# Batch 1 in aligned key sets, one-operation activation for batch 0, global values copied on chip

## The chip, the cores and the metric

One of the eight cores of a Trainium2 chip. The metric is the device time of one execution in microseconds. An execution is timed without the profiler several times; one more is taken with it, and all lines of views come from that one.

## The reference

Eight batches of attention with eight heads of width 64: 512 local tokens see the keys within 32 positions and all 32 global keys; 32 global tokens see everything. The joined result goes through a hidden layer of 2,048 with a sigmoid gate.

```python
k_all = np.concatenate([k_g, k_l], axis=2)
v_all = np.concatenate([v_g, v_l], axis=2)
out_g = np.matmul(sm(scale * np.matmul(q_g, k_all.transpose(0, 1, 3, 2))), v_all)
s_ll = np.where(np.abs(pos[:, None] - pos[None, :]) <= 32, scale * (q_l @ k_l^T), -1e9)
a_l = sm(np.concatenate([scale * (q_l @ k_g^T), s_ll], axis=-1))
out_l = np.matmul(a_l, np.concatenate([v_g, v_l], axis=2))
x = np.concatenate([out_g, out_l], axis=2)      # to tokens x 512
h = x @ w_in                                    # 4352 x 2048
out = (h * (1.0 / (1.0 + np.exp(-1.702 * h)))) @ w_out
```

Inputs and output are float32; the matmuls run on bf16 operands.

## The kernel before

**Units.** A batch is done as two quads of four heads (`a` and `c`). In a quad the four heads lie on the four groups of 32 partitions, so that four score matmuls with 32 rows of contraction stand in the array together, one for each head. Scores go to two pairs of PSUM banks (`psS`), everything else to four banks that go round (`psP`): hidden layer `hp`, output `op`, values `ov`.

**Two forms of attention.** `Quad` (batches 0 and 1) has keys as rows and takes its local scores in four blocks of 128 keys with windows of queries (`WIN`). `S` makes scores, `X` exponentials, `M` multiplies by the near mask (batch 1 only; batch 0 adds a bias in PSUM instead, `B`). The global keys go apart: `K` makes their scores, `XK` the exponentials `ek`, `ekU` their part of the sum. In batch 1's first quad `XK` also makes `ek2`, `ek` with its partition groups turned by one, with two SyncE DMAs (`load_turned`); `rvt` is the global values turned in the same way. Values are the weights of the matmuls in `U`, exponentials the moving side, so the sums come out transposed; `R` turns the row of sums, inverts it and turns it back, `XL` multiplies. `Gm` and `G` do the global tokens.

`Wide` (batches 2 to 7) uses key sets of 128 rows: 96 local keys and the 32 global keys beside them (`spread` copies keys into that layout, on ScalarE; `ext` puts the global ones in). Here the exponentials are the weights and the values move, 66 columns wide with a column of ones (`UG`); `RXG` normalises on VectorE and transposes. Local keys start at three offsets, so the values are needed at three alignments: `vt` as loaded, and two turned copies `vturn`, made by `turn_v` with four SyncE DMAs. `load_v` loads five blocks of 96 local values, each followed by a DMA of the same global values beside it, and a last block of 32.

**Activation.** gelu-like gate as h * (1 + tanh(0.851 h)) / 2: tanh on ScalarE (`th`), then a VectorE operation (th + 1) * hp to `gT`; the factor 0.5 is in the copy of the output (`o_out`). `act4` does the same for 4 steps of batch 0 that wait in the `psS` banks.

**Order.** Written out by hand; every engine runs its instructions in program order. Batch 0's attention; its hidden layer (16 steps `fc` of 4 matmuls); then batch 0's output projection (`osteps`, 16 groups of 4 matmuls) with batch 1's attention between; batch 1's hidden layer with the start of batch 2's attention; then `phase_o(i)` and `phase_h(i)` alternate: output of batch i with attention of batch i+1, hidden layer of batch i+1. Global tokens of all batches come last.

**Loads.** The loads from DRAM that cast to bf16 are issued by GpSimd (POOL) in one queue, in the order of `load_rest`, then `load_v(2)`, then `loads(i)` in hidden layer i. Output copies and turned values are issued by SyncE (SP). `keep` is 28 matmuls on zeros at the start, before there is data.

Of the kernel before, what the change touches and what calls it, by code (L numbers as in the profile page):

```python
# [20 lines left out]
def kernel(  # L21
# [67 lines left out]
    def load_v(b):  # L89
        vt = v_rows(b)  # L90
        if b < 4:
            nc.gpsimd.memset(vt[:, :, :, D:], 1.0)
        vs, vg = (x[b].rearrange("h s d -> s h d") for x in (v_l, v_g))
        for c in range(5):
            nc.gpsimd.dma_start(out=vt[0:96, c, :, :D], in_=vs[96 * c : 96 * c + 96])  # L95
            nc.gpsimd.dma_start(out=vt[96:128, c, :, :D], in_=vg)  # L96
        nc.gpsimd.dma_start(out=vt[0:32, 5, :, :D], in_=vs[480:512])

# [11 lines left out]
    rvg = consts.tile([128, 4, D + 2], BF16)  # L110


    rvt = consts.tile([128, 4, D + 2], BF16)
# [5 lines left out]
    def load_g(lo, hi, names="kqv"):  # L119
        for name, dst, src in (("k", rkg, kgf), ("q", rqg, qgf)):  # L120
            if name in names:
                nc.gpsimd.dma_start(out=dst[:, lo:hi, :], in_=src[:, lo:hi, :])
        if "v" in names:
            load_turned(nc.gpsimd, rvg[:, lo:hi, :D], vgf[:, lo:hi, :])
# [33 lines left out]
    for i in range(2):  # L158
        vtiles.append(consts.tile([128, 8 * 6 * (D + 2)], BF16, name="v%d" % i))
        nc.gpsimd.memset(v_view(i, 4)[:, :, :, :, D:], 1.0)  # L160
# [25 lines left out]
    keep(28, psP.tile([128, 512], F32, name="w", tag="p"), 128)  # L186

    qtiles = []
    for i in range(4):
        qt = consts.tile([128, 24, 32], F32, name="q%d" % i)  # L190
        nc.vector.memset(qt[:, 0:4, :], 0.0)
        nc.vector.memset(qt[:, 20:24, :], 0.0)
        qtiles.append(qt)

    WIN = ((0, 10), (6, 12), (14, 12), (22, 10))
    near_mask = consts.tile([128, 2, LW], BF16)
# [15 lines left out]
    def make_near(c):  # L212
        nr = WIN[c][1]
        at = (0, 160, 0, 192)[c]
        nc.scalar.activation(near_mask[:, c // 2, at : at + 16 * nr].rearrange("p (t r) -> p t r", t=16),
                             near(bandt, c), AF.Copy)

# [5 lines left out]
    def mask_put(g, first, last, by, late):  # L223
# [22 lines left out]
    qgT = consts.tile([128, 4, 40], F32)  # L246
    nc.vector.memset(qgT[:, :, 32:], 0.0)
    kgT = consts.tile([128, 4, 32], F32)
# [12 lines left out]
    def load_rest():  # L261
        load_v2(0)
# [5 lines left out]
        for g4 in (1, 0, 2, 3):  # L268
            nc.gpsimd.dma_start(
                out=w_out_sb[:, 4 * g4 : 4 * g4 + 4, :].rearrange("p (g e) m -> p g (e m)", e=2),  # L270
                in_=w_out_r[:, 2 * g4 : 2 * g4 + 2, :])
            if g4 == 0:
                load(1, (0,))
                load_g(2, 4)
        load(1, (1,))
        load(2, kq=False)
        nc.gpsimd.dma_start(out=loaded[2][1][:, 0], in_=qf[2][:, 0])
        load_g(4, 8, "k")
        load_v2(1)
        load_g(4, 8, "q")  # L280
        nc.gpsimd.dma_start(out=loaded[2][0], in_=kf[2])
        nc.gpsimd.dma_start(out=loaded[2][1][:, 1], in_=qf[2][:, 1])
# [14 lines left out]
    class Quad:  # L297
        def __init__(self, Q):
# [5 lines left out]
            self.v = v_view(self.b, 4 if self.b < 2 else 5)[:, self.u]  # L304
            if self.b < 2:
# [43 lines left out]
        def S(self, rnd, split=False, added=False, part=None):  # L349
# [19 lines left out]
            if not part:  # L369
                self.E[rnd] = att.tile([128, 4, RW + 32], BF16, name="e%d" % rnd)  # L370
# [29 lines left out]
        def M(self, rnd):  # L400
            at = 36 if rnd else 40
            e = self.E[rnd][:, :, at : at + LW]
            nc.vector.tensor_mul(e, e, near_mask[:, rnd : rnd + 1, :].to_broadcast([128, 4, LW]))

# [25 lines left out]
        def XK(self, two=True):  # L430
            self.ek = att.tile([128, Sl], BF16, name="ek")
            nc.scalar.activation(self.ek, self.kb, AF.Exp, scale=scale)
            self.ek2 = None
            if two:
                self.ek2 = att.tile([128, Sl], BF16, name="ek2")
                load_turned(nc.sync, self.ek2, self.ek)

        def ekU(self, unit, warm=0, ov=None):
# [4 lines left out]
            for j in range(4):  # L443
                two = unit == 1 and self.ek2 is not None
                r = 32 * ((j + 1 + two) % 4)
                p = slice(r, r + 32)
                lv = (ones32[p] if unit == 0 else
                      (rvt if two else rvg)[p, self.Q, :D].rearrange("p (w h) -> p w h", h=2)[:, :, unit - 1])
                nc.tensor.matmul(ov[32 * j : 32 * j + 32, :], lhsT=lv, rhs=(self.ek2 if two else self.ek)[p],  # L449
                                 start=True, stop=False, skip_group_check=True)  # L450

        def ekUs(self, nxt=None, rnd=0, banks=(None, None, None)):
# [5 lines left out]
            if self.ek2 is not None:  # L458
                self.ekU(1, ov=banks[1])
            if nxt:  # L460
                nxt.K(1)
            if self.ek2 is None:
                self.ekU(1, ov=banks[1])
# [76 lines left out]
    class Wide(Quad):  # L540
# [9 lines left out]
        def spread(self):  # L550
# [3 lines left out]
            nc.scalar.activation(self.kg4[:, :, 0:96], kl[:, 0:480].rearrange("p (m w) -> p m w", m=5), AF.Copy)  # L554
            nc.scalar.activation(self.kT[:, 640:672], kl[:, 480:512], AF.Copy)
# [15 lines left out]
        def S(self, rnd):  # L571
# [14 lines left out]
            self.E[rnd] = att.tile([128, 4, LW], BF16, name="e%d" % rnd)  # L586
# [13 lines left out]
        def UG(self):  # L600
            self.ov = []
            for lo, hi in self.BANKS:
                ov = pbank("ov")
                self.ov.append(ov)
                work = []
                for t in range(lo, hi):
                    w = min(max(t, 1), 14)
                    work.append((t // 8, t + 1 if t < 8 else t - 8, w, 128, t - lo))
                if hi == 16:
                    work += [(*g, 4) for g in OUTER]  # L610
                for i, (rnd, o, w, n, to) in enumerate(work):
                    rho, m = at_of(w)
# [25 lines left out]

    gTs, ops = {}, {}
# [12 lines left out]
    def h_act(i, fc, hp):  # L652
        n = width(i)
        th = moe.tile([128, TB], F32, name="th", bufs=4)
# [23 lines left out]
    def o_out(i, tci, op):  # L678
        ob = moe.tile([128, d_model], F32, name="ob", bufs=6)
        last = i == B and tci == B // 4 - 1  # L680
        for lo, hi in ((0, 320), (320, 512)) if last else ((0, 512),):
# [5 lines left out]
            nc.scalar.activation(ob[:, lo:hi], op[:, lo:hi], AF.Copy, scale=0.5)  # L687
            for j in range(4):
                eng = nc.scalar if last and j % 2 else nc.sync
                if 2 <= i < B:  # L690
# [8 lines left out]

    def act4(i, hf):  # L700
        f = slice(2 * hf, 2 * hf + 2)
        nc.vector.scalar_tensor_tensor(gTs[i][:, f, :], in0=th4s[i][:, f], scalar=1.0, in1=pts[i][hf],
                                       op0=ALU.add, op1=ALU.mult)

    pts, th4s = {}, {}
# [39 lines left out]
    a.XK(False)  # L745
# [5 lines left out]
    c.XK(False)  # L751
# [12 lines left out]
    pt = pts[0] = spair()  # L764
# [17 lines left out]
    th4 = th4s[0] = early  # L782

    def tanh2(hf):
        f = slice(2 * hf, 2 * hf + 2)
        nc.scalar.activation(th4[:, f], pt[hf], AF.Tanh, scale=0.851)

    tanh2(0)
    c.G()
    act4(0, 0)  # L790
    for fc in range(4, FC):
        h_step(0, fc)
        if fc in (5, 6, 8, 9):
            make_near((5, 6, 8, 9).index(fc))
        if fc == 12:
            tanh2(1)
            act4(0, 1)
# [8 lines left out]
    load_turned(nc.sync, rvt[:, 2:4], rvg[:, 2:4])  # L806
    nq = {1: (Quad(2), Quad(3)), 2: (Wide(4), Wide(5))}
    a, c = nq[1]
    a.T()
    transpose_g(2, 4)  # L810
    a.ext()
    osteps(0, (0, 1), (0, 0), (1, 1), (1, 0), (2, 1))
    a.S(0)
    a.gg()
    a.K()
    a.X(0)
    a.XK()
    a.M(0)
    a.eg()
    c.T()  # L820
    c.ext()
    osteps(0, (2, 0), (0, 2), (0, 3))
    a.S(1)
    a.X(1)
    a.M(1)
    osteps(0, (1, 2), (1, 3))
    c.S(0)
    c.X(0)
    c.M(0)
    osteps(0, (2, 2), (2, 3))  # L830
    c.S(1)
    a.ekUs(c, 1)
    c.X(1, lambda: c.XK(False))
# [175 lines left out]
```

## Time and profile before

| | us |
|---|---|
| median of 3 runs | 297.59 |
| lowest, highest | 297.01, 298.99 |
| profiled execution | 297.65 |
| its span | 295.9 |

The span is from the first to the last instruction; 1.75 us lie around it. The granted TensorE clock was 1.00. Stretches of the profile, by the start of their first matmul:

| stretch | from, us |
|---|---|
| batch 0's hidden layer | 19.15 |
| batch 0's output with batch 1's attention | 33.86 |
| batch 1's hidden layer | 55.50 |
| batch 1's output with batch 2's attention | 71.50 |
| batch 2's hidden layer | 89.41 |
| batch 3's hidden layer | 121.76 |

PE is TensorE's matmuls, PEld its weight loads, DVE VectorE, ACT ScalarE, POOL GpSimd, SP SyncE; L12 is line 12 of the kernel. A name such as `gT<-th,hp` says what is written from what. In a timeline a line has start, duration, engine, line, operation, and in brackets the engine's idle time before it and what ended it. The chain of waits is followed back from the last instruction, at each step to what released it.

### The profile page before, as it was taken

Reading aid. Unit: us, or ns where it says so; the run is one execution under the profiler, and the core shown is the slowest. Engines: PE = TensorE matmul, PEld = TensorE weight load, DVE = VectorE, ACT = ScalarE, POOL = GpSimd, SP = SyncE. Lnnn points to the kernel's source line nnn. Section 1 sums busy time; section 2 is a strip of 40 time slices with the busy share of each in tenths; the row PEclk is TensorE's granted clock in tenths of the full one; section 3 lists DMA queues with packets and bytes.
Section 4 is the critical chain, followed back from the end, with each engine's and each line's share of the span. In section 5 each row is a group of like instructions: output and inputs, shape, how many; then the busy total and the mean of one; then the engine's idle time right before and its main releaser. Section 6 shows DMA issues by size and latency. Waiting matters only on the chain.

```text
span 295.9 us, 9591 instructions
## 1 busy us (share of the span) xinstructions
PE 282.7 (96%) x4076; PEld 145.0 (49%) x4129; DVE 200.7 (68%) x409; ACT 161.4 (55%) x282; POOL 84.4 (29%) x151
## 2 busy tenths in 40 slices
PE   7799999999999999999999999999999999999994
PEld 6354434444554455445454445444544454456553
DVE  6587956997968876777767767787678654773310
ACT  4727567277546645566547734764556551763421
POOL 6853556584504240162107130353000000000000
PEclk9999999999999999999999999999999999999999
DMA  7999999989934992299527992399226012101123
GB/s 196 153 177 210 194 190 212 169 155 210 139 76 115 229 104 67 72 188 193 80 55 153 222 102 55 82 235 151 65 59 181 2 47 65 38 0 35 39 62 80
DMA packets 63418, 35.94 MB, mean 121 GB/s; under 512 B 49808, under 2 KB 52240, under 8 KB 63376
## 3 DMA queue, kind: packets, MB, share of 16 engines
q0 software_dynamic: 53296, 17.77, 56.1%
q1 hardware_dynamic: 9328, 16.85, 20.4%
q10 hardware_dynamic: 752, 0.72, 0.8%
q8 instruction: 32, 0.52, 0.8%
q14 instruction: 10, 0.08, 0.1%
HBM read 36.70 MB, written 8.91 MB: 154 GB/s over the span
## 4 chain that ended last, share of the span: by engine, by line
PE 86%; DMA 5%; DVE 3%; issue 2%; ACT 2%; ACTq 0%; POOL 0%; SPq 0%; DVEq 0%
PE hp L648 38%; PE op L673 35%; PE s L581 5%; PE ov L614 4%; DMA ek<-ek 2%; DMA rk<-in_k_l_dram 2%; PE s L648 1%; ACT e L396 1%; DMA early<-in_k_l_dram 1%; DVE xL L508 1%; PE ov L475 1%; PE op L685 1%; PE s L363 1%; PE ov L449 0%; DVE rs L503 0%
## 5 line engine op out<-in xcount | busy, mean ns | idle before, releaser
L673 PE MATMUL op<-w_out_sb,gT 128*128 128x512 bf16 x486 | 119.1, 380 | 3.5 <-issue 2.1
L656 DVE SCALAR_TENSOR_TENSOR gT<-th,hp 128x512 bf16<-128x512 f32 (+1 forms) x140 | 90.3, 655 | 35.3 <-ACT th L655 34.3
L648 PE MATMUL hp<-xL,w_in_sb 128*128 128x512 bf16 x487 | 108.3, 379 | 0.9 <-DVE xL L508 0.2
L655 ACT ACTIVATE th<-hp 128x512 f32<-128x512 f32 (+1 forms) x140 | 79.1, 572 | 43.2 <-PE hp L648 42.9
L648 PEld LDWEIGHTS <-w_in_sb 128*128 128x128 bf16 x576 | 56.1, 98 | 64.9 <-issue 1.1
L673 PEld LDWEIGHTS <-gT 128*128 128x128 bf16 x528 | 48.3, 98 | 52.4 <-issue 1.4
L590 ACT ACTIVATE e<-s 128x704 bf16<-128x704 f32 x48 | 33.7, 755 | 24.5 <-PE s L581 24.5
L687 ACT ACTIVATE ob<-op 128x512 f32<-128x512 f32 (+2 forms) x35 | 20.5, 585 | 46.2 <-PE op L673 39.8
L596 DVE TENSOR_TENSOR e<-e,mask 128x1024 bf16<-128x1024 bf16 (+1 forms) x24 | 17.4, 724 | 22.4 <-ACT e L590 22.4
L95 POOL DMA_DIRECT2D v<-in_v_l_dram x30 | 23.6, 786 | 23.5 <-PE hp L648 14.1
L96 POOL DMA_DIRECT2D v<-in_v_g_dram x30 | 17.7, 590 | 18.3 <-DMA rk<-in_k_l_dram 14.9
L628 DVE TENSOR_TENSOR xn<-ov,rc 128x384 bf16<-128x384 f32 (+1 forms) x36 | 19.5, 542 | 1.2
L168 POOL CAST tick<-gT 1x1 f32<-1x1 bf16 x5 | 0.9, 174 | 59.8 <-DVE gT L656 59.8
L581 PEld LDWEIGHTS <-kT 32*128 32x128 bf16 x1344 | 12.4, 92 | 10.2 <-issue 9.3
L396 ACT ACTIVATE e<-s 128x856 bf16<-128x856 f32 x14 | 11.7, 881 | 7.3 <-PE s L363 7.3
L581 PE MATMUL s<-q,kT 32*128 32x32 bf16 (+2 forms) x1344 | 15.2, 184 | 0.0
L627 DVE RECIPROCAL rc<-ov 128x6 f32<-128x6 f32 (+1 forms) x36 | 6.6, 183 | 9.8 <-PE ov L614 9.8
L614 PEld LDWEIGHTS <-e 128*32 128x32 bf16 (+1 forms) x1056 | 10.1, 94 | 5.1 <-DVE kl L547 2.1
L547 DVE STREAM_TRANSPOSE kl<-rk 128x512 f32<-128x512 f32 x12 | 12.4, 1034 | 0.1
L560 DVE STREAM_TRANSPOSE q<-rq 128x512 f32<-128x512 f32 x12 | 12.5, 1039 | 0.0
L614 PE MATMUL ov<-v,e 128*32 128x66 bf16 (+1 forms) x528 | 11.0, 197 | 0.0
L614 PE MATMUL ov<-vt,e 128*32 128x66 bf16 x528 | 10.4, 195 | 0.0
(110 smaller groups left out, 187.6 us busy)
## 6 DMA issues: line engine op xcount, KB each, us to landing
out_dram<-ob SPq DMA_DIRECT2D x132, 64.0 KB, 2.0
vt<-v SPq DMA_DIRECT2D x12, 264.0 KB, 8.7
rk<-in_k_l_dram POOLq DMA_DIRECT2D x6, 512.0 KB, 11.7
vt<-v SPq DMA_DIRECT2D x6, 495.0 KB, 5.0
v<-in_v_l_dram POOLq DMA_DIRECT2D x30, 96.0 KB, 9.3
rq<-in_q_l_dram POOLq DMA_DIRECT2D x5, 512.0 KB, 8.3
w_in_sb<-in_moe_w_in_dram POOLq DMA_DIRECT2D x8, 256.0 KB, 9.0
w_out_sb<-in_moe_w_out_dram POOLq DMA_DIRECT2D x4, 512.0 KB, 10.5
```

The costliest lines, as they stand in the source:

```text
L95: nc.gpsimd.dma_start(out=vt[0:96, c, :, :D], in_=vs[96 * c : 96 * c + 96])
L96: nc.gpsimd.dma_start(out=vt[96:128, c, :, :D], in_=vg)
L581: nc.tensor.matmul(bank(self.ps, j)[:, 0:LW].rearrange("p (t q) -> p t q", q=32)[:, os], lhsT=self.k[p, k0 : k0 + 128, e], rhs=self.q[p, t ...
L590: nc.scalar.activation(self.E[rnd][:, 2 * i : 2 * i + 2, :], self.ps[i][:, :, :LW], AF.Exp, scale=scale)
L596: nc.vector.tensor_mul(e, e, m.to_broadcast([128, 4, n]))
L614: nc.tensor.matmul(ov[32 * j : 32 * j + 32, 66 * to : 66 * to + 66], lhsT=self.E[rnd][0:n, j, 32 * o : 32 * o + 32], rhs=self.vs[rho][0:n, ...
L628: nc.vector.tensor_mul(xn[:, lo // 2 : hi // 2].rearrange("p a h w b -> p a b h w"), o3[:, 0:n, 0:D].rearrange("p (a b) (w h) -> p a b h w ...
L648: nc.tensor.matmul(hp[:, : width(i)], lhsT=w_in_c[:, fc // 4, kc, fc % 4 // 2, :, fc % 2], rhs=(xL[i] if i < B else xG)[:, kc, :], start=( ...
L655: nc.scalar.activation(th[:, :n], hp[:, :n], AF.Tanh, scale=0.851)
L656: nc.vector.scalar_tensor_tensor(gTs[i][:, fc, :n], in0=th[:, :n], scalar=1.0, in1=hp[:, :n], op0=ALU.add, op1=ALU.mult)
L673: nc.tensor.matmul(op, lhsT=gTs[i][:, fc, tci * 128 : tci * 128 + 128], rhs=w_out_sb[:, fc, :], start=(first and fc == 4 * f4), stop=(fc = ...
L687: nc.scalar.activation(ob[:, lo:hi], op[:, lo:hi], AF.Copy, scale=0.5)
```

## The change

- Batch 1 is done by a new class `Near`, in the manner of `Wide`, with key sets that start at multiples of 128 rows of the layout, so that only values as loaded are needed and no turned copy. Its scores fill 512 columns a head in each round, its exponentials are masked in `XM`, and `parts` lists which blocks go into which output tile. `near_mask` for it is made by `mask_near` on GpSimd. `ek2`, `rvt` and `M` go.
- Batch 0's activation is one ScalarE operation, `Gelu_apprx_sigmoid`, from PSUM to `gT`; `act4` and the tanh of four steps go; the output copy of batch 0 has no factor.
- Global values are loaded once (beside block 0) and copied on VectorE to the other four blocks (`spread_v`), before `turn_v`.
- Loads: batch 1's queries and keys come before `w_out`'s parts 0, 2, 3; batch 1's values come through `load_v(1)`, between parts 2 and 3; batch 2's queries and keys in whole DMAs.
- Exponentials lie in one constant tile `ebuf`; `Tq` of batch 2's first quad moves into batch 1's hidden layer; the hidden layer of batch 1 starts with four steps in the `psS` banks.
- The warming matmuls are 20 of 128 columns and 68 of 96 columns with 32 rows, over four banks.

```diff
     def load_v(b):
         vt = v_rows(b)
+        if b == 1:
+            nc.gpsimd.memset(vt[:, 5], 0.0)
...
+        nc.gpsimd.dma_start(out=vt[96:128, 0, :, :D], in_=vg)
         for c in range(5):
             nc.gpsimd.dma_start(out=vt[0:96, c, :, :D], in_=vs[96 * c : 96 * c + 96])
-            nc.gpsimd.dma_start(out=vt[96:128, c, :, :D], in_=vg)
         nc.gpsimd.dma_start(out=vt[0:32, 5, :, :D], in_=vs[480:512])
+        if b == 1:
+            nc.gpsimd.dma_start(out=vt[96:128, 5, :, :D], in_=vs[480:512])
+
+    def spread_v(b):
+        vt = v_rows(b)
+        nc.vector.tensor_copy(vt[96:128, 1:5, :, :D], vt[96:128, 0:1, :, :D].to_broadcast([32, 4, 8, D]))
...
-    keep(28, psP.tile([128, 512], F32, name="w", tag="p"), 128)
+    cold = [psP.tile([128, 512], F32, name="w", tag="p") for _ in range(4)]
+    keep(20, cold[0], 128)
+    for i in range(68):
+        p = slice(32 * (i % 4), 32 * (i % 4) + 32)
+        nc.tensor.matmul(cold[i % 4][:, 0:96], lhsT=warm[p, 0:128], rhs=warm[p, 0:96], start=True, stop=True)
...
+    def mask_near():
+        def zero(lo, hi, first, last, by):
+            nc.gpsimd.memset(near_mask[lo:hi, first:last:by], 0.0)
+
+        nc.gpsimd.memset(near_mask, 1.0)
+        zero(0, 96, 4, 24, 5)
+        zero(0, 96, 24, 27, 1)
+        for g, first, late in ((1, 0, True), (0, 1, False), (2, 1, True), (1, 2, False), (2, 3, False), (0, 4, True)):
+            mask_put(g, first, 24, 5, late, near_mask)
...
         load_v2(0)
...
-        for g4 in (1, 0, 2, 3):
...
+        w_out(1)
+        load(1, (0,))
+        mask_near()
+        load_g(2, 4)
         load(1, (1,))
...
+        w_out(0)
+        w_out(2)
+        load_v(1)
+        w_out(3)
+        load(2)
+        load_g(4, 8)
...
-        def UG(self):
+        def UG(self, ps=None):
...
+    NEAR = (
+        ((0, 0, 5, 0), (128, 3, 5, 5), (128, 17, 1, 15), (256, 6, 5, 10)),
+        ((384, 9, 5, 0), (384, 17, 1, 14), (512, 12, 5, 5), (512, 17, 1, 15), (256, 17, 1, 13), (544, 15, 3, 10)),
+    )
+
+    class Near(Wide):
+        def S(self, rnd):
+            self.ps = spair()
+            for k0, lo, n, o in NEAR[rnd]:
+                for e in range(2):
+                    for j in range(4):
+                        p = slice(32 * j, 32 * j + 32)
+                        nc.tensor.matmul(
+                            bank(self.ps, j)[:, 32 * o : 32 * o + 32 * n],
+                            lhsT=self.k[p, k0 : k0 + 128, e], rhs=self.q[p, lo : lo + n, :, e],
...
+        def XM(self, rnd):
+            lo, n, at = ((1, 14, 0), (0, 13, 14))[rnd]
+            m = near_mask[:, at : at + n].rearrange("p (a t) q -> p a (t q)", a=1)
+            for i in range(2):
+                e = self.E[rnd][:, 2 * i : 2 * i + 2]
+                nc.scalar.activation(e, self.ps[i], AF.Exp, scale=scale)
+                e = e[:, :, 32 * lo : 32 * lo + 32 * n]
+                nc.vector.tensor_mul(e, e, m.to_broadcast([128, 2, 32 * n]))
+
+        def parts(self, t):
+            if t == 16:
+                return [(0, 0, 0, 0, 128), (0, 15, 0, 1, 96), (1, 13, 0, 2, 96), (1, 14, 0, 3, 96),
+                        (1, 15, 0, 4, 96), (1, 12, 0, 5, 128)]
+            work = []
+            for m in range(5):
+                d = t - 3 * m
+                if -1 <= d <= 3:
+                    o = (d + 1 if m == 0 else 5 * m + d + 1 if m < 3 else 16 + 5 * (m - 3) + d + 1)
+                    work.append((o // 16, o % 16, 0, m, 128 if 0 <= d < 3 or t == 15 else 96))
+            if t >= 14:
+                work.append((1, t - 4, 0, 5, 128))
+            return work
...
     def h_act(i, fc, hp):
         n = width(i)
+        if i == 0:
+            nc.scalar.activation(gTs[i][:, fc, :n], hp[:, :n], AF.Gelu_apprx_sigmoid)
+            return
...
-    tanh2(0)
+    for hf in range(2):
+        nc.scalar.activation(gTs[0][:, 2 * hf : 2 * hf + 2], pt[hf], AF.Gelu_apprx_sigmoid)
     c.G()
-    act4(0, 0)
+    nq = {1: (Near(2), Near(3)), 2: (Wide(4), Wide(5))}
+    a, c = nq[1]
+    a.Tk()
+    a.spread(nc.vector.tensor_copy)
+    a.Tq()
+    a.ext()
     for fc in range(4, FC):
         h_step(0, fc)
...
+    osteps(0, (0, 1), (1, 1))
     a.S(0)
+    a.XM(0)
+    c.Tk()
+    c.spread(nc.vector.tensor_copy)
+    c.Tq()
     c.ext()
+    osteps(0, (2, 1), (3, 1), (0, 0))
     a.S(1)
+    a.XM(1)
+    osteps(0, (1, 0), (2, 0), (3, 0))
     c.S(0)
+    c.XM(0)
+    spread_v(1)
+    osteps(0, (0, 2), (1, 2))
     c.S(1)
+    c.XM(1)
+    osteps(0, (2, 2), (3, 2))
+    a.UG(spair())
+    a.RXG()
+    osteps(0, (0, 3), (1, 3), (2, 3))
+    c.UG()
+    c.RXG()
+    osteps(0, (3, 3))
...
+    pt = spair()
+    hps = [bank(pt, fc) for fc in range(4)]
+    for kcs in ((0, 1), (2, 3)):
+        for fc in range(4):
+            h_mm(1, fc, hps[fc], kcs)
     for fc in range(FC):
...
         if fc == 5:
             a.spread()
+            a.Tq()
         if fc == 7:
             a.ext()
         if fc == 8:
+            spread_v(2)
             turn_v(2)
...
             if fc == 6 and i + 1 < B:
+                spread_v(i + 1)
                 turn_v(i + 1)
```

## The prediction

> **What bounds the kernel now.** First the busy times, on the page:
>
> ```profile
> PE 282.7 (96%) x4076; PEld 145.0 (49%) x4129; DVE 200.7 (68%) x409; ACT 161.4 (55%) x282; POOL 84.4 (29%) x151
> ```
>
> TensorE is nearly always occupied, so a gain must take matmuls away or close its gaps. Next the chain of waits over the stages that the change rebuilds, batch 0's output projection with batch 1's attention and then batch 1's hidden layer (columns: start, duration, what):
>
> ```profile
> 32.99 0.86 PE hp L648 x4
> 33.86 3.67 PE op L673 x17
> ...
> 41.64 6.70 DMA ek<-ek
> ...
> 55.76 1.30 DVE xL L508 x2
> 57.05 0.04 issue
> 57.10 0.39 PE hp L648
> ...
> 70.94 0.56 PE s L581 x56
> 71.50 0.32 PE op L673
> ```
>
> A matmul of 512 columns costs 0.2165 us (0.86 for four). From 33.86 to 71.50 there are 64 of the output and 64 of the hidden layer, 27.7 us, and two score rounds of batch 2 at 0.56; some 8.8 us are batch 1's attention and waits. The waits are the turned copy of `ek` and VectorE's tail (transposes, `xL`) before 57.10.
>
> Then VectorE's timeline in batch 1's hidden layer, and SyncE's issues of the turned values beside it:
>
> ```profile
> 61.49 3.22 DVE L656 SCALAR_TENSOR_TENSOR gT<-th,hp 128x512 bf16<-128x512 f32 x5
> ```
>
> ```profile
> 61.18 0.54 SPq L102 DMA_DIRECT2D vt<-v  x1
> ...
> 63.80 0.59 SPq L105 DMA_DIRECT2D vt<-v  x1
> ```
>
> VectorE needs 0.644 a step (3.22/5) where TensorE needs 0.866: little room. The four turned copies are issued as soon as the values are there. Their landing, first in the stretch 61 to 65 beside loads of q and k, then in 222 to 226 with no load beside them:
>
> ```profile
> DMA to landing us min/median/max: 4.4/7.8/8.1
> DMA to landing us min/median/max: 4.5/4.6/5.1
> ```
>
> From the first issue to the last landing that is at most 63.80 + 8.1 - 61.18 = 10.7 us, against 224.8 + 5.1 - 222.3 = 7.6 alone. The same four beside loads at 92.2 and 125.2 give 10.9 and up to 13.6.
>
> **The change, part by part.**
>
> *Scores and values of batch 1.* A round of `Wide` (L581) has 14 groups of four row-tiled matmuls, 704 columns, in 0.56; a round of `Quad` (L363) 4 groups, 856 columns, in 0.61. A line through both gives 0.0057 a group and 0.69 ns a column. `Near` has 8 and 12 groups of 1,024 columns: 0.75 and 0.77. L614 takes 88 matmuls in 0.87; `Near` has 128: 1.27. For two quads 3.04 + 2.54 = 5.6 us, in place of the 8.3 us that the old attention took up to the hidden layer (57.10 less five matmuls is 56.0; 56.0 - 33.86 - 13.86).
>
> Walk from 33.86: 8 output matmuls to 35.6; S to 36.35; two exponentials of 1,024 columns (the tanh of that size took 1.02) end at 38.4; 12 matmuls to 38.95; S to 39.7; 12 to 42.3; c's S to 43.1, exponentials to 45.1, 8 matmuls to 44.8, a wait of 0.4 for the banks; S to 45.95, exponentials to 48.0, 8 matmuls to 47.7, a wait of 0.4; values to 49.4; 12 matmuls to 52.0; values to 53.25; 4 matmuls to 54.1. The hidden layer's first half takes 1.73, to 55.85; c's normalised values are there 3.75 after 52.0 (75.06 to 78.40 in batch 2, and 0.4 for the longer matmuls). So it starts at 54.1 in place of 56.0: 1.9 us gained.
>
> *Loads.* The timeline of POOL shows that each load is issued when the eighth before it has landed, and by those waits a part of `w_out` takes 2.45 us of the queue (29.90, 32.38), half of a q or k 1.25 (33.57, 34.82). In the new order: first half of q and k at 30.9 and 32.1, second 35.1, `w_out` part 0 37.5 (wanted 38.1), part 2 40.0 (wanted 43), values by 44 to 46 (wanted 48.1), part 3 46.5 to 48.5 (wanted 49.4). I take nothing; the covers are 0.6 to 3 us, and what is later than that shows one to one. `mask_near`, some 16 small POOL operations (a memset of 576 took 0.60, the others 0.1 to 0.4), 4 us, falls between issues where POOL sat waiting 1.24, 0.88 and 1.72 before; with eight loads outstanding the queue stays fed: nothing, or up to 1 if it starves.
>
> *Batch 0's activation.* Fourteen VectorE products (12 of 0.644, two of 1.2) leave. TensorE set that stage (23.39 to 33.86 are 48 matmuls at 0.218): nothing. The products covered nothing else; a's transposes take their place on VectorE, waiting for k at 32.1 and done by 35.3, and nobody is queued behind them. The function change needs tables: the only load in the trace, at 2.24, took 1.28. One more fits into ScalarE's 4.73 idle before 22.28; the second between the last activation (about 34.4) and the first exponential at 36.35: covered by 0.7. The Trainium skill (ScalarE: Activation LUTs, What ACT_TABLE_LOAD costs) counts a drain of about 1.38 on top of 1.28 for every change of set; the trace agrees on the 1.28 and shows no second load. By that rule the first exponential would be late by about 0.7 and the sum below 0.3 to 0.7 higher.
>
> *Batch 1's hidden layer.* VectorE now has Tk and Tq (0.89 each from start to start), ext (0.45) and `spread_v` inside it. The copy (2,048 bf16 elements on 32 partitions) is in no row. Casts of 128 and 512 elements took 0.23 and 0.40, which gives 1.1; the f32 products of 256 and 384 (0.45, 0.59) give 2.4. I take 1.1, as the cast is the nearest operation. The Trainium skill (VectorE: DVE Perf Modes, The perf-mode tier table) has 693 ns for a copy of 2,048 bf16 elements; by that the sum is 0.4 lower; no run here shows it yet. First product at 57.0; nine of them, Tk, Tq and ext end at 65.0, the copy at 66.1. TensorE has four banks, so steps 10 and 13 wait on VectorE: the second score round ends at 70.2, where without these waits it would be 54.1 + 13.86 + 1.12 = 69.1. Before, 71.50: gain 1.3.
>
> *Turned values.* `turn_v(2)` waited for the load alone, at 61.18; now for `spread_v`, first issue 66.2. Behind it in SyncE's queue are output copies that come later anyway; the one who waits is TensorE at `UG`, 70.2 + 3.47 = 73.7. By then the large q and k loads (issued from about 58) have landed and small value pieces are beside it, so I take 8.0, nearer to 7.6 than to 10.7: 74.2, 0.5 late. Kept: 0 to 3.2.
>
> *Batches 3 to 7.* A hidden layer starts at 89.41, step 6's product ends 7.4 later, so the first issue moves from +2.75 to +8.6. `UG` wants it at +17.9 (107.34). With 8.0 it lands at +16.6: 1.3 spare. The copy's 1.1 on VectorE is inside the four banks' slack (2.6 us from a step's end to the reuse of its bank, 1.35 of it used). Four value loads of 0.58 POOL time fewer per batch free nothing on the path. Nothing.
>
> *Start.* Twenty warming matmuls at 0.106 (28 took 4.54 - 1.57) and 68 row-tiled ones: 0.7 us at L581's rate, 7.3 if each cost a full one. I take 1.4, twice L581's rate, since matmuls there still ran at half rate (128 columns in 0.106). The scores then start up to 0.3 later, covered by 1.39 of idle TensorE before 12.30, which waits for k's transpose at 11.21; uncovered beyond 1.4. The new masks and memsets lie off the chain.
>
> *Sum.* 1.3 - 0.5 = 0.8. The profiled execution took 297.65 (span 295.9 and 1.75 around it), against a median of 297.59: 297.65 - 0.8 = **296.9**.
>
> **Rivals.**
>
> *Faster by over 1%.* VectorE keeps up and the turned values are in time: the score round ends at 69.1, and if the two bank waits go too, at 68.3, 3.2 gained: **294.4**. For it: the copy may be shorter than 1.1. Against: nine products and three transposes before it are rows.
>
> *Slower: the turned values become the bound.* One mechanism, in five hidden layers: SyncE's issue sits behind `spread_v` on VectorE, and `UG` waits. It decides from a first-issue-to-last-landing of 9.3 us on (17.9 - 8.6). At 10.5 it costs 4 x 1.2 and 3.0 in batch 2 (the last batch has no load beside it), less the 1.3: **304.2**. For it: every turn beside loads took 10.7 or more. Against: those were issued together with q and k, which are 5 us ahead now.
>
> *Near no change by late weights.* `w_out` or the values of batch 1 come 1 to 2 us late, at the first wants of the new order, and eat the gain: **298.2**. For it: a cover of only 0.6 at part 0. Against: the spacing is the queue's own, and the output copies leave that stretch.
>
> *The warming does not warm.* If the 68 small matmuls keep the clock at half, as the first 28 show it before about 5.5, the chain from 12.3 to 19.2 and the first 16 projections stretch: 3 to 4 us, **301**.
>
> **How the numbers follow.** Forecast 0.48 (295 to 298.5), late weights 0.12, faster 0.20, turned values 0.16, no warming 0.04. A measurement of this kernel can't tell less than about 1%, 3 us, from no change: faster than 294.6 gets 0.21 (the fast rival and the forecast's edge), slower than 300.6 gets 0.18, within 0.61. The range leaves out about a tenth on either side: 294.2 to 301.5.
>
> **What would show it.** Right: no `ek` DMA in the chain; the hidden layer of batch 1 starts near 54; two more table loads with no wait for them; `spread_v` near 1.1; its issue of turned values near 66, and TensorE idle for under 1 us at L614's first use of `vt`. Wrong: `UG` waiting for `vt` in batches 3 to 6; output matmuls waiting for `w_out`; the score round's end outside 69 to 71.

## The result and the profile after

| | us |
|---|---|
| changed, median of 4 runs | 318.84 |
| lowest, highest | 317.61, 324.87 |
| before, median of 4 runs beside them | 297.3 |
| ratio, 95% interval | 1.071 (1.063 to 1.078) |

The change makes the kernel 7% slower, 21 us. Ratios, here and below, are of fast runs alone: a run more than 1.5% above the fastest of its kernel, such as the 324.87 here, counts in the median but not in the ratio. The profile shown here is that of a second profiled execution of the changed kernel (321.33, span 319.6); the first one, at 324.87, has the same five waits for `vt`. Busy times, from the page:

```profile
PE 287.8 (90%) x4294; PEld 147.1 (46%) x4349; DVE 195.5 (61%) x400; ACT 162.6 (51%) x276; POOL 76.7 (24%) x142
```

TensorE is busy 5 us longer than before, with a share of 90 in place of 96%, and with 218 more matmuls; the lower clock told of below is part of these 5 us. What it waited for (columns: who, its line, what for, us in total, times, longest):

```profile
PE ov L622 <- DMA vt<-v: 10.8, 5, 2.9
PE ov L622 <- issue: 3.6, 2, 2.0
PE op L729 <- issue: 3.1, 17, 0.3
PE ov L481 <- issue: 2.1, 1, 2.1
```

Before, the list had no wait for `vt` and no wait over 0.4 that the profile puts down to "issue" (nothing that it shows). L622 is `UG`, L481 batch 0's values.

The chain of waits from the second quad's values of batch 1 through batch 1's hidden layer to batch 2's values:

```profile
53.54 0.54 PE ov L622 x52
54.08 1.98 issue
56.06 0.82 PE ov L622 x72
...
58.70 3.38 PE s L701 x12
...
71.09 0.70 DVE v L105
...
74.87 8.73 DMA vt<-v
83.60 0.04 issue
83.64 1.00 PE ov L622 x75
```

Where the chain of before ran on TensorE through this stretch, it now leaves it: VectorE's products and transposes, the copy of the global values (L105), SyncE's issues, and 8.73 us of the last turned copy, for which `UG` waits until 83.64.

In batches 3 to 6 it is the same. VectorE and then SyncE in batch 2's hidden layer, which starts at 99.35, and below them the time from an issue to its landing:

```profile
106.94 0.71 DVE L105 COPY v<-v 32x2048 bf16<-32x2048 bf16 x1
107.69 2.68 DVE L712 SCALAR_TENSOR_TENSOR gT<-th,hp 128x512 bf16<-128x512 f32 x4
```

```profile
107.79 0.55 SPq L110 DMA_DIRECT2D vt<-v  x1
...
109.78 0.65 SPq L113 DMA_DIRECT2D vt<-v  x1
```

```profile
DMA to landing us min/median/max: 8.3/9.1/9.5
```

From 107.79 to 109.78 + 9.5 = 119.3 are 11.5 us. Over the hidden layers, worked out from issues and landings in the trace (us after the layer's first matmul):

| values of batch | first issue | last landing | took | wait at `UG` |
|---|---|---|---|---|
| 2 | 13.36 | 25.11 | 11.75 | 2.15 |
| 3 | 8.44 | 19.89 | 11.45 | 1.63 |
| 4 | 8.47 | 20.00 | 11.53 | 1.74 |
| 5 | 8.45 | 20.64 | 12.19 | 2.39 |
| 6 | 8.36 | 21.17 | 12.81 | 2.88 |
| 7 | 8.36 | 15.62 | 7.26 | none |

Only batch 7, with no load beside its turn, is in time.

A second loss stands behind the first. TensorE's granted clock was 1.00 throughout before. Now it falls four times, each time to 0.50 for 3.41 us. Each fall is shown below the 3.41 us ahead of it, and last comes a stretch with a wait behind which the clock did not fall (columns: stretch, length, busy us of each engine with its instructions, then the clock, the DMA share and GB/s; the first busy time is TensorE's):

```profile
53.32:56.73 3.41, 1.43 (x130) 1.16 (x128) 1.12 (x6) 0.60 (x1) 2.84 (x13) 1.00 1.17 149
56.73:60.14 3.41, 3.08 (x24) 1.22 (x13) 2.01 (x6) 0.60 (x1) 0.13 (x1) 0.50 0.36 82
80.63:84.04 3.41, 1.13 (x62) 0.62 (x62) 0.06 (x1) 0.60 (x1) 0.00 (x0) 1.00 0.54 119
84.04:87.45 3.41, 3.19 (x54) 1.48 (x42) 3.31 (x10) 0.00 (x0) 0.00 (x0) 0.50 0.24 55
152.31:155.72 3.41, 0.74 (x67) 0.64 (x68) 1.44 (x4) 0.46 (x2) 0.00 (x0) 1.00 0.76 90
155.72:159.13 3.41, 3.11 (x16) 1.19 (x16) 1.55 (x5) 0.00 (x0) 0.00 (x0) 0.50 0.11 25
223.99:227.40 3.41, 0.53 (x62) 0.42 (x54) 0.08 (x1) 1.12 (x3) 0.00 (x0) 1.00 1.23 160
227.40:230.81 3.41, 3.19 (x54) 1.46 (x40) 2.80 (x9) 0.00 (x0) 0.00 (x0) 0.50 0.11 25
189.86:193.27 3.41, 1.60 (x79) 1.14 (x81) 1.25 (x4) 0.41 (x2) 0.00 (x0) 1.00 0.79 104
193.27:196.68 3.41, 3.25 (x74) 1.58 (x77) 1.95 (x7) 1.41 (x2) 0.00 (x0) 1.00 0.02 5
```

A fall costs at most 0.50 x 3.41 = 1.7 us, the four 6.8. In this trace it follows a stretch in which TensorE was busy for 0.53 to 1.43 of 3.41 us, 16 to 42%; behind 1.60, 47%, it did not come. (In the other traces shares of 41 to 46% stand on both sides.) The four starts lie 8, 21 and 21 times 3.41 us apart, so the stretches follow a fixed grid. By these cases it counts how much of one stretch a wait empties: the waits of 1.98, 2.15 and 2.88, and those of 1.74 and 1.59 together, cost clock, and the one of 2.39, divided differently by the grid, did not. The Trainium skill (TensorE: Matmul & The Clock Gate, Part 1) says that TensorE falls to half its clock after an idle window of some 3.4 us. The trace agrees on the half rate and on the length, but here the window did not have to be idle throughout.

So the span's 319.6 - 295.9 = 23.7 us are: 10.8 waiting for `vt`, at most 6.8 of clock, and 3.6 + 2.1 of long waits for nothing that the profile shows, 23.3 together. The smaller items, of both signs, nearly cancel.

### The profile page after: what moved, and what is told of

Its sections match the earlier page's. It is cut to its first block, busy times and chain, and to the rows that moved or that the text cites. A ratio compares the mean times of both kernels' runs of the same rounds, so it can differ in the third digit from the quotient of the medians.

```text
span 323.2 us, 9986 instructions
## 1 busy us (share of the span) xinstructions
PE 290.5 (90%) x4294; PEld 148.1 (46%) x4349; DVE 195.9 (61%) x400; ACT 162.5 (50%) x276; POOL 76.7 (24%) x142
## 4 chain that ended last, share of the span: by engine, by line
PE 68%; DMA 18%; issue 4%; DVE 4%; SPq 3%; ACT 2%; ACTq 0%; POOL 0%
PE op L729 31%; PE hp L701 24%; DMA vt<-v 15%; PE ov L622 4%; PE s L588 3%; PE s L701 2%; DMA rq<-in_q_l_dram 2%; DVE gT L712 2%; SPq L112 1%; DMA early<-in_k_l_dram 1%; SPq L111 1%; PE s L660 1%; PE op L741 1%; PE ov L481 1%; ACT th L711 1%
## 5 line engine op out<-in xcount | busy, mean ns | idle before, releaser
L729 PE MATMUL op<-w_out_sb,gT 128*128 128x512 bf16 x484 | 124.9, 394 | 6.2 <-issue 3.3
L712 DVE SCALAR_TENSOR_TENSOR gT<-th,hp 128x512 bf16<-128x512 f32 (+1 forms) x124 | 78.7, 651 | 29.4 <-ACT th L711 28.1
L711 ACT ACTIVATE th<-hp 128x512 f32<-128x512 f32 (+1 forms) x124 | 69.6, 569 | 38.7 <-PE hp L701 38.4
L598 ACT ACTIVATE ebuf<-s 128x704 bf16<-128x704 f32 x48 | 33.7, 755 | 45.3 <-PE s L588 43.1
L604 DVE TENSOR_TENSOR ebuf<-ebuf,mask 128x1024 bf16<-128x1024 bf16 (+1 forms) x24 | 17.4, 724 | 30.3 <-ACT ebuf L598 30.3
L622 PEld LDWEIGHTS <-ebuf 128*32 128x32 bf16 (+1 forms) x1312 | 13.3, 98 | 22.5 <-DMA vt<-v 12.0
L622 PE MATMUL ov<-vt,ebuf 128*32 128x66 bf16 x528 | 11.9, 201 | 11.4 <-DMA vt<-v 11.4
L622 PE MATMUL ov<-v,ebuf 128*32 128x66 bf16 (+1 forms) x656 | 13.7, 201 | 3.9 <-issue 3.9
L642 DVE STREAM_TRANSPOSE xL<-xn 128x512 f32<-128x512 f32 x14 | 9.8, 701 | 0.0
L674 ACT ACTIVATE ebuf<-s 128x1024 bf16<-128x1024 f32 x8 | 7.8, 1021 | 4.0 <-PE s L660 4.0
```

The lines of the kernel that those rows point to most:

```text
L598: nc.scalar.activation(self.E[rnd][:, 2 * i : 2 * i + 2, :], self.ps[i][:, :, :LW], AF.Exp, scale=scale)
L604: nc.vector.tensor_mul(e, e, m.to_broadcast([128, 4, n]))
L622: nc.tensor.matmul(ov[32 * j : 32 * j + 32, 66 * to : 66 * to + 66], lhsT=self.E[rnd][0:n, j, 32 * o : 32 * o + 32], rhs=self.vs[rho][0:n, ...
L711: nc.scalar.activation(th[:, :n], hp[:, :n], AF.Tanh, scale=0.851)
L712: nc.vector.scalar_tensor_tensor(gTs[i][:, fc, :n], in0=th[:, :n], scalar=1.0, in1=hp[:, :n], op0=ALU.add, op1=ALU.mult)
L729: nc.tensor.matmul(op, lhsT=gTs[i][:, fc, tci * 128 : tci * 128 + 128], rhs=w_out_sb[:, fc, :], start=(first and fc == 4 * f4), stop=(fc = ...
```

## The experiments

The theory after the result: the turned copies are issued 5 us later, since they wait for a VectorE copy that stands behind seven products, and in that place they take 12 us and not 8, because value loads share the transfers; TensorE waits for them and then runs for a while at a lower clock. The rivals: the loss is that of the unshown waits and of more TensorE instructions; or the turn is slow in this kernel wherever it starts. Times below are the median; ratios are against the kernel before on the same chip (median 297.1 to 297.3).

### The copy earlier

```diff
+    spread_v(2)
     for fc in range(FC):
...
-            spread_v(2)
             turn_v(2)
...
+        if i + 1 < B:
+            spread_v(i + 1)
         for fc in range(FC):
...
-                spread_v(i + 1)
                 turn_v(i + 1)
```

> The changed kernel, with the copy of the global values put on VectorE before a hidden layer's first product in place of behind its seventh (ninth in batch 1's). Nothing else moves. Theory (the turned copies start too late, because SyncE's issue waits for a VectorE copy that stands behind seven products, and TensorE then waits for them and runs at a lower granted clock for a while): the first issue goes back to about 2.5 us after the hidden layer's start, the last landing to at most 16.5 after it even if a turn takes 13.6, the waits for vt go, and the time falls from 318.8 to 296 to 302 (what is left is the 2 us by which batch 0's hidden layer and the 2.3 us by which the stretch with batch 1's attention came late in the profile, at most 5). Rival (the waits in which TensorE waits for nothing that the profile shows, 3.9 us at the value matmuls, and more instructions are behind most of the loss): stays above 308. Rival (the turn simply takes longer in this kernel, whenever it starts): 304 to 310, waits for vt remain.

Measured: 305.0 (302.04 to 307.55), ratio 1.015 (1.008 to 1.022), which is 301.7 on 297.2. The first issue is at 3.6 to 3.7 us, the turn takes 11.1 to 12.9, its last landing is at most 16.5 after the layer's start, and no wait for `vt` is left; the longest in the list is now this:

```profile
PE ov L622 <- issue: 4.5, 2, 2.3
```

The profiled execution, at 307.55, is the longest of the four; its clock fell three times (from 12.67, 57.04 and 149.20), at most 5.1 us.

Moving one VectorE operation takes back some 17 of the 21 us. That the turn takes 12 here too refutes a turn that is slow only in the changed place; in the kernel before it also took 10.7 to 13.1, and started early enough.

### Five loads again

```diff
-        nc.gpsimd.dma_start(out=vt[96:128, 0, :, :D], in_=vg)
         for c in range(5):
             nc.gpsimd.dma_start(out=vt[0:96, c, :, :D], in_=vs[96 * c : 96 * c + 96])
+            nc.gpsimd.dma_start(out=vt[96:128, c, :, :D], in_=vg)
...
-            spread_v(2)
```

> The changed kernel with the global values loaded five times, one beside each block, as before the change; no copy on VectorE. The place of the turned copies in the program is the same. Theory (late issue): like the kernel with the early copy, 296 to 302; a difference of over 1 us between the two is the price or worth of the four extra loads by themselves. Rival (unshown waits and more instructions): above 308. Rival (turn longer in this kernel): 304 to 310.

Measured: 305.66 (303.58 to 307.26), ratio 1.025 (1.019 to 1.032). The waits for `vt` are gone; the turns start 3.6 us after the layer's start (5.8 in batch 1's) and take 12.4 to 14.2 beside loads. It is above the expected range. The profiled execution, the longest of the four, has a wait that the changed kernel does not have:

```profile
PE op L729 <- DMA w_out_sb<-in_moe_w_out_dram: 2.7, 1, 2.7
```

In the changed order of loads batch 1's values stand ahead of the last part of `w_out`, and here four more small loads stand there too. So the single load is worth something in that stretch, up to 2.7 us with the new order in this execution; in batches 2 to 7 no worth shows.

### The copy alone in the kernel before

```diff
+        nc.gpsimd.dma_start(out=vt[96:128, 0, :, :D], in_=vg)
         for c in range(5):
             nc.gpsimd.dma_start(out=vt[0:96, c, :, :D], in_=vs[96 * c : 96 * c + 96])
-            nc.gpsimd.dma_start(out=vt[96:128, c, :, :D], in_=vg)
...
+            spread_v(2)
             turn_v(2)
...
+                spread_v(i + 1)
                 turn_v(i + 1)
```

> The kernel before, with only this part of the change: the global values of batches 2 to 7 loaded once and copied on VectorE behind step 8 or 6 of the hidden layer, just ahead of the turned copies. Theory (late issue): five hidden layers each put the first issue 5 us later, a turn of 12 then lands 2 to 3 us after the value matmuls want it, and the lower clock after the wait about doubles that: 297.3 + 5 x 3 to 5 = 312 to 320. Rival (it is the other parts of the change): 297 to 300.

Measured: 312.45 (311.56 to 313.41), ratio 1.049 (1.043 to 1.054).

```profile
PE ov L618 <- DMA vt<-v: 12.8, 6, 3.2
```

This part alone costs 15 us. The clock fell twice, from 78.18 and from 149.86, 3.4 us; with 12.8 of waits that is 16.2, less 1.7 by which this execution was ahead when batch 1's hidden layer began (53.83 against 55.50), near the span's 14.9.

### Value loads later

```diff
             load(i + 2)
             if i == 1:
                 load_g(8, NQ)
-            load_v(i + 2)
+
+    def late_v(i):
+        if i + 2 < B:
+            after(gTs[i][:, 12])
+            load_v(i + 2)
...
             if fc == 6 and i + 1 < B:
                 spread_v(i + 1)
                 turn_v(i + 1)
+            if fc == 12:
+                late_v(i)
```

> The changed kernel with the copy where the change has it, but with the value loads of batch i+2 issued behind step 12 of hidden layer i in place of step 0, so that no value load runs beside the turned copies. If the turn of 12 us is the work of the value loads beside it, the turn takes 7.6 to 9 from first issue to last landing, TensorE waits for vt under 1 us in each batch, and the time is 298 to 304. If the turn is slow in itself when it starts that late, or because of the q and k loads, it stays at 11 or more and the time above 312.

Measured: 300.34 (298.52 to 302.67, 10 runs), ratio 1.011 (1.008 to 1.015). The copy stays where the change has it, the first issue is again at 8.4, and the turn takes 7.9 to 9.1. The transfers during one turn, first in the changed kernel (108 to 120), then here (99 to 108); q0 holds the loads from DRAM, q1 the turned copies and the output:

```profile
DMA packets 5049, 2.27 MB, mean 189 GB/s; under 512 B 4559, under 2 KB 4559, under 8 KB 5048
...
q0 software_dynamic: 4683, 0.97, 94.4%
```

```profile
DMA packets 2289, 1.88 MB, mean 209 GB/s; under 512 B 1823, under 2 KB 1823, under 8 KB 2288
...
q0 software_dynamic: 1968, 0.65, 65.2%
```

The rates are near each other; what differs is how much moves beside the 1.2 MB of the turned copies. (These rates are means over the windows themselves, so bytes over rate gives back the length of the window and is no forecast of it.) This is the cleanest answer to the question: the same late issue brings no wait for `vt` if most of the value loads are not beside it.

### Both, and what is left

The remaining 1 to 1.5% over the kernel before was looked for with both moves as the base.

> The changed kernel with both moves: the copy of the global values ahead of the hidden layer's first product, and the value loads of batch i+2 behind step 12. Theory (late turned copies are the whole loss of batches 2 to 7): no wait for vt; with the start and the stretch of batch 1's attention as they are, 297 to 301, at most 1 us under the kernel with late value loads alone (300.5), since that one shows no such wait either. Rival (the late value loads now collide with something else): above 302.

Measured: 302.26 (301.46 to 302.59), ratio 1.015 (1.012 to 1.018). Not under the kernel with late values alone: the early copy stands in a hidden layer where VectorE is full, and batch 1's output now waits 1.2 for `gT`. That is not all of the difference: this execution's clock was 0.50 from 13.82 to 17.23, up to 1.7 of the 2.0 us by which its batch 0's hidden layer starts later (21.90 against 19.92).

This kernel also tells what lengthens a turn. Its value loads are late, and yet its turns in batches 2 to 6 take 12.1 to 14.1 us: they start some 5 us earlier, when more of q and k is still to come. The transfers during one of them, 162.49 to 174.56 (view of 162 to 174):

```profile
DMA packets 979, 2.34 MB, mean 195 GB/s; under 512 B 177, under 2 KB 177, under 8 KB 979
...
q0 software_dynamic: 562, 0.99, 52.9%
```

There are 177 pieces under 512 B here and 4,559 in the changed kernel, beside nearly the same 0.99 and 0.97 MB of loads, in turns of 12.1 and 11.5 us. So how much is loaded beside a turn shows in its length, and the size of the pieces does not decide it. Over all turns of all kernels, with the loads counted that began between first issue and last landing: 7.2 to 8.1 us beside none, 7.9 to 9.1 beside 0.4 to 0.7 MB, 10.7 to 14.2 beside 0.75 to 1.44 MB.

The next kernels take up the waits put down to "issue". With the old warming:

```diff
-    keep(20, cold[0], 128)
-    for i in range(68):
...
+    keep(28, psP.tile([128, 512], F32, name="w", tag="p"), 128)
```

> As the kernel with both moves, with the warming matmuls of before (28 of 128 columns; 120 TensorE instructions fewer). Theory (the waits of TensorE for nothing that the profile shows come from its own instructions, which arrive in pieces of 16 KB, 256 instructions: a wait in the trace ends about 1.4 us after such a piece has arrived, and comes where a dense run of small matmuls meets the end of a piece): the 0.9 to 1.0 us at batch 0's second quad (value matmuls before batch 0's hidden layer) goes, since the pieces end elsewhere, and batch 0's hidden layer starts about 1 us earlier, at 18.7 to 19.2; the wait in batch 1's values moves or changes. Total 0 to 1.5 us less than with both moves alone. Rival (the waits come from loads that contend at that moment): both waits stay where they are, same time.

Measured: 300.98 (300.23 to 301.62), ratio 1.012 (1.008 to 1.016); batch 0's hidden layer starts at 18.56 (21.90 with both moves alone, up to 1.7 of the difference by the clock), and its wait of 0.4 is gone. But a wait of 2.6 now stands in the first quad's values of batch 1.

With output matmuls between the banks:

```diff
-    osteps(0, (2, 2), (3, 2))
-    a.UG(spair())
+    a.UG(spair(), ((2, 2), (3, 2), None))
     a.RXG()
-    osteps(0, (0, 3), (1, 3), (2, 3))
-    c.UG()
+    osteps(0, (0, 3), (1, 3))
+    c.UG(None, ((2, 3), (3, 3), None))
     c.RXG()
-    osteps(0, (3, 3))
```

> As the kernel with both moves, with batch 1's value matmuls cut in their three banks and four output matmuls of 0.87 us put between the banks, so that the 256 instructions of a quad's values are spread over some 3 us in place of 1.4. Theory (instruction pieces): the wait of 1.7 to 2.3 us in the second quad's values falls to under 0.7, and the kernel gains 1 to 2 us over both moves alone. Rival (contending loads, or the second quad's data): the wait stays over 1.5.

Measured: 301.1 (299.98 to 301.62), ratio 1.011 (1.008 to 1.015). The wait in the second quad falls from 1.99 to 1.28, less than expected.

> As the kernel with both moves, with the old warming and with output matmuls between the banks of batch 1's values. By the theory of instruction pieces 295.5 to 298, the fastest of these; by the rival the same as with both moves alone.

Measured: 300.1 (298.79 to 301.5), ratio 1.009 (1.006 to 1.012). The lowest ratio of all, though not to be told from its neighbours, and not the 295.5 to 298 of the theory.

Late value loads with the old warming, without the early copy:

> The changed kernel with the late value loads (copy where the change has it) and the warming matmuls of before. With the new warming the late value loads alone gave 300.5; the old warming let batch 0's hidden layer start at 18.5 to 18.6 in place of 19.9 to 21.9. Theory (the new warming costs the start 1 to 2.5 us, by its own length and by the instruction pieces): 298 to 299.5. Rival (a start that is earlier only waits longer for the loads of batch 1's stretch, which set its end): 300 to 301, batch 1's hidden layer still from 56 on.

Measured: 301.52 (300.97 to 302.16), ratio 1.014 (1.011 to 1.018). A miss: batch 0's hidden layer starts at 18.89, but the wait in batch 1's first quad is 3.2, and batch 1's hidden layer starts at 57.60, later than the 55.74 with the new warming.

```diff
     a.RXG()
...
+    nq[2][0].Tq()
     c.RXG()
...
             a.spread()
-            a.Tq()
```

> As the kernel with late value loads and old warming, with the transpose of q for batch 2's first quad (1.04 us on VectorE) moved out of batch 1's hidden layer, to a place where VectorE waits for the second quad's values. If VectorE's load in that hidden layer is what makes it 0.9 us longer than before the change (34.7 from its start to batch 2's, against 33.8), the wait of 1.1 us for the product gT goes and the time falls by 0.8 to 1.1. If the transfers or TensorE set that stretch: no change.

Measured: 300.75 (299.29 to 303.58), ratio 1.013 (1.006 to 1.019), not to be told from the one before it. The wait of 1.1 for `gT` stays, so this transpose is not its cause.

> As the one before it (late value loads, old warming, q transposed earlier), with output matmuls between the banks of batch 1's values. The candidate for the fastest: if the three costs add up (start 1 to 2, instruction pieces 1, VectorE 0.9) 296.5 to 298. If batch 1's stretch is set by its loads: 299 to 301 as with the others.

Measured: 300.94 (299.96 to 301.62), ratio 1.013 (1.009 to 1.017). No version beats the kernel before.

What the waits are can be read from the places where they stand. TensorE's timeline at batch 1's values (`s` or `ov` are the two quads; in brackets the idle time before), with both moves:

```profile
49.54 0.70 PE L622 MATMUL s<-v,ebuf 128*32 128x66 bf16 x65
50.72 0.71 PE L622 MATMUL s<-v,ebuf 128*32 128x66 bf16 x63 [0.48 <-issue]
51.36 2.76 PE L729 MATMUL op<-w_out_sb,gT 128*128 128x512 bf16 x11
54.05 0.60 PE L622 MATMUL ov<-v,ebuf 128*32 128x66 bf16 x53
56.65 0.81 PE L622 MATMUL ov<-v,ebuf 96*32 96x66 bf16 x75 [1.99 <-issue]
```

and with the old warming (here the kernel with q transposed earlier):

```profile
46.65 1.23 PE L618 MATMUL s<-v,ebuf 128*32 128x66 bf16 x125
50.59 0.21 PE L618 MATMUL s<-v,ebuf 128*32 128x66 bf16 x3 [2.71 <-issue]
50.73 2.76 PE L725 MATMUL op<-w_out_sb,gT 128*128 128x512 bf16 x11
53.43 1.22 PE L618 MATMUL ov<-v,ebuf 128*32 128x66 bf16 x113
55.96 0.30 PE L618 MATMUL ov<-v,ebuf 96*32 96x66 bf16 x15 [1.31 <-issue]
```

The waits moved from behind matmul 65 and 53 of the 128 to behind 125 and 113: by 60 in both quads. The old warming has 28 matmuls in place of 88, 60 fewer. So these waits stand at a fixed number of instructions from the program's start, whatever is there, and from one to the next are 63 + 12 + 53 = 128 matmuls with their weight loads, 256 instructions. The other traces agree: every wait of a matmul of 0.4 us or more that is put down to "issue", in any of the kernels, stands behind 351, 734, 862, 1,757 or 2,269 recorded weight loads, which are 3, 1, 7 and 4 times 128 apart to within one. The page of the changed kernel has the transfers that go with it:

```profile
q8 instruction: 34, 0.56, 0.7%
```

34 packets of 16 KB, for some 8,700 TensorE instructions. In the traces such a packet mostly takes 0.9 to 1.6 us (2.5 at most), and TensorE goes on 1.2 to 1.6 us after its end. The Trainium skill (Runtime: NRT & Kernel Launch, Instruction fetch mechanics) says the same of the size, 256 instructions in a block of 16 KB, and that crossing a boundary is mostly hidden. The traces agree on the size; it was not hidden here. From boundary to boundary it took 56.65 - 50.72 = 5.9 us and 55.96 - 50.59 = 5.4, where the instructions between needed 3.9 and 4.1. In the kernel before, no such wait was over 0.4, although there too some 256 instructions lie in 3.0 us (75.0 to 78.0: 134 matmuls and 135 weight loads). So density alone does not decide whether there is a wait; what else must come together was not found.

That these waits make up the whole remaining 1% was not shown. They sum to 2.6 to 4.4 us in the profiles of the eight kernels with late value loads, beside losses of 2.7 to 4.5 us by the ratios, but spreading the matmuls took only part of them away, and where batch 1's stretch would end without them was not measured. In three of the eight profiles (both moves, old warming, and late values with old warming) a fall of the clock took up to 1.7 us too.

### The changed kernel once more

> The changed kernel once more, unaltered, for a second profile of it (the first profiled execution took 324.87, 6 more than the median of the four). If the late turned copies set the time of batches 2 to 7, this profile again shows first issues 8.4 us after a hidden layer's start, 11.6 to 13 us to the last landing, a wait for vt of 1.8 to 3.2 in batch 2 to 6 and none in batch 7, and hidden layers 34.5 to 36 us apart as in the kernel before with the late copy alone; a total of 317 to 320.

Measured: 321.33 (one run; the kernel before took 298.14 beside it). That is above the 317 to 320 expected. Its waits are those shown above, the two shortest 1.6 and 1.7, under the 1.8 expected. From batch 2's hidden layer on, they are 34.1, 37.5, 34.8 and 36.9 us apart; the two beyond the expected 36 are those where the clock fell.

## Why the prediction was wrong, by its steps

**Turned values and batches 3 to 7: the step that failed.** What failed is the forecast "I take 8.0, nearer to 7.6 than to 10.7" for the time from the first issue of a turn to its last landing. It measured 11.5 to 12.8 beside loads. The first issue was right (8.4 after the start against 8.6, and in batch 2 13.4 against 12.1), and so was `UG`'s want (18.1 against 17.9), so the rival that the turned values become the bound, given 0.16, had its place and its decision point of 9.3 right: all five hidden layers with loads wait, the sixth does not. The reason for 8.0 was that q and k would have landed and only small value pieces be left. In batch 2's turn it was so: all of the 0.75 MB loaded beside it were pieces under 512 B, and it still took 11.75. In batches 3 to 6 it was not quite so: of the 1.0 MB beside a turn 0.56 were value pieces and the rest q and k. So the small pieces were counted as next to nothing (8.0 against 7.6 alone), where they weigh about as much as other loads. With most of them gone, at the same late issue, the turn took 7.9 to 9.1.

**The term that was missing.** The rival's price, 304.2, counted waits alone, at 10.5. It had 4 x 1.2 and 3.0, 7.8 us of them, and 10.8 were measured. The clock's 6.8, three of its four falls behind these waits, was in no step, nor were the instruction waits.

**Scores and values of batch 1.** The gain of 1.9 us did not come. From the first output matmul to batch 1's hidden layer 20.24 were forecast; the execution with late value loads took 55.74 - 33.90 = 21.84, the kernel before 55.50 - 33.86 = 21.6. Its score rounds took 3.2 (3.04) and the values 3.1 (2.54), and an instruction wait of 1.7 came on top, while the two bank waits of 0.4 did not occur. More instructions had been priced by their run time only.

**Start.** That the longer warming is covered was wrong too: batch 0's hidden layer started at 19.9 to 21.9 in the executions with it and at 18.0 to 19.2 with the old one, by 0.8 at its beginning (5.30 against 4.54, where the forecast's own terms, 20 x 0.106 + 1.4 less 2.97, give 0.55 and not its 0.3), an instruction wait of 0.4 to 2.1, and, in the kernels with the early copy alone and with both moves, a fall of the clock near 13, 1.7. The executions also differ among themselves by the landing of the first q (8.4 to 11.2); how much is whose was not separated.

**Right.** The loads: the changed kernel has no wait for `w_out` or for batch 1's values, though the kernel with five loads shows how thin that cover was. The activation: two table loads with no wait for either.

```profile
35.77 0.60 ACT L708 ACTIVATE gT<-hp 128x512 bf16<-128x512 f32 x1 [0.27 <-PE hp L701]
36.38 1.28 ACT L674 ACT_TABLE_LOAD   x1
38.09 1.94 ACT L674 ACTIVATE ebuf<-s 128x1024 bf16<-128x1024 f32 x2 [0.42 <-PE s L660]
```

The table load begins 0.01 after the last activation ends and the first exponential then waits for TensorE. The Trainium skill (ScalarE: Activation LUTs, What ACT_TABLE_LOAD costs) adds a drain of about 1.38 to a change of set; this trace does not show it. The copy took 0.69 to 0.71 and not the 1.1 worked out from the casts; the 693 ns of the Trainium skill (VectorE: DVE Perf Modes, The perf-mode tier table) agree with the trace. That batch 1's hidden layer is limited by VectorE held in part: TensorE waits 1.12 and 0.18 there for `gT`. From its start to the end of the second score round 16.1 were forecast; 17.8 were measured in the changed kernel, 0.8 of it by the clock, and 17.0 with late values. Taking the transpose of q out of it shortened it to 16.5, by the smaller of the two waits and a little more.

## What to carry to other kernels

A transfer that is moved has to be priced with the bytes that are loaded beside it at its new place: the same turned copies took 7.2 to 8.1 us beside nothing, 7.9 to 9.1 beside 0.4 to 0.7 MB, and 10.7 to 14.2 beside 0.75 to 1.44 MB, where the forecast took 8.0 because the pieces beside them would be small. An operation that seems free on a busy engine (0.7 us on VectorE) costs what stands ahead of it in that engine's order for whoever waits on it, here 5 us of issue. And a wait of 2 to 3 us on TensorE can cost nearly twice its length, because the clock may fall after it.

## What was not expected of the hardware

- After a stretch of 3.41 us in which waits left TensorE busy for 16 to 42%, the granted clock was 0.50 for the next 3.41 us, at most 1.7 us lost each time; after 47% it was not. The stretches lie on a fixed grid.
- TensorE's own instructions arrive 256 at a time. Some runs of small matmuls that use 256 in about 4 us met waits of up to 3.2 us at the boundary, and others as dense met none; 60 matmuls fewer at the start of the program moved the waits by 60 matmuls.
- The turned copies of 1.2 MB were lengthened by loads beside them as much when these were 177 pieces under 512 B and the rest large as when they were 4,559 (12.1 and 11.5 us, beside 0.99 and 0.97 MB).
